# One visit a pair, on 64x64 quarters, for pairs 13 to 24 too

## The chip, the cores and the metric

The kernel runs on one core of a Trainium2 chip. The metric is the device time of the core in microseconds (us), a median over runs. The core's engines have a queue each and run it in order: TensorE (PE, matmuls), VectorE (DVE), ScalarE (ACT), GpSimd (POOL), and SyncE (SP), which issues DMAs.

## The reference

Attention with RMS-normalized queries and keys, followed by a feed-forward network with squared ReLU, in float32 (the weights arrive as float64):

```python
def _attn_ref(q, k, v, g_q, g_k):          # (8, 12, 448, 64) each
    rmsnorm = lambda x, g: x / np.sqrt(np.mean(x * x, axis=-1, keepdims=True) + 1e-06) * g
    q_n, k_n = (rmsnorm(q, g_q), rmsnorm(k, g_k))
    scores = 1.0 / np.sqrt(q.shape[-1]) * np.matmul(q_n, k_n.transpose(0, 1, 3, 2))
    attn = np.exp(scores - np.max(scores, axis=-1, keepdims=True))
    attn = attn / (np.sum(attn, axis=-1, keepdims=True) + 1e-09)
    return np.matmul(attn, v)
def _moe_ref(x, w_in, w_out):              # (3584, 768), (768, 2048), (2048, 768)
    h = np.maximum(x @ w_in, 0.0)
    return (h * h @ w_out)
# between them: x = attn_out.transpose(0, 2, 1, 3).reshape(3584, 768)
```

## The kernel before

**Work.** The 8 x 12 heads are 48 pairs of heads of one batch, 6 pairs a batch. The keys of a head are 448 = 3 x 128 + 64: three full slots and a half one, and the half slots of an even pair and of the odd pair behind it share one tile, scored with the even pair. Scores are made with keys on partitions. ACT turns them into weights with an exponential that applies the scale (`weigh`, L466), POOL adds a pair's weight tiles into one sum a head (`add_up`, L485), PE sums these over partitions by a matmul with ones (`denominators`, L620), DVE transposes the result (`take_sums`, L662) and inverts it (L679, L680). The values product (`attend`, L550, for the full slots; L586 for the half ones) is multiplied by that inverse in `finish`.

**Units.** The feed-forward network works on two batches at a time, a unit of four blocks. A block has first products (L1021 in the first unit, L1077 in later ones), whose results DVE combines (L1163) and ACT squares (L1169, L1170), sums of hidden parts on POOL (L1186), and second products (L1200 for the rest of the rows, L1286 for the others), whose results DVE adds up (L1383). The first unit uses seven products in place of eight; the later units go one level deeper. During the first unit the weights are converted as well: ACT (L1443 to L1446, "words") and DVE (L1457, L1476) make float32 of the words that DMAs bring, and DVE and POOL make their sums, the forms (L1552). DVE also makes sums of the input weights for the later units (L1512, "more").

**Visits.** Work on attention is done in visits between product passes. Pairs 0 to 12 are done alone, ahead of the first unit. The visit of pair i holds the scores of pair i and the values product of pair i - 1. For pairs 13 to 24, in the first unit, there are two visits a pair (`visit_among`), at every 24th of the unit's cost: in the first, slots 0 and 1 are attended (L550) and scored (L458), in the second the rest; the separate `denominators(i - 1)` stand half a step ahead of the second one, or in it where it is the unit's second step. From pair 25 on there is one visit (`visit_whole`), in which attending (L565) and scoring (L447) alternate slot by slot, each matmul cut into 64 by 64 quarters: the values product goes to two banks, one for the upper and one for the lower halves of the keys, which `join_halves` adds afterwards (L576 to L578). Denominators are made there for two pairs at once at the head of an even visit (`both_denominators`, L629).

**Banks.** The eight PSUM banks appear in the lists below as bank_172 to bank_179 (0 to 7). Products take turns on 5, 6 and 7 (`roles`). `visit_among` scores into banks 0 to 3, has the denominators in bank 3 and the values in bank 4. A whole visit has the values in 4 and 3, the denominators in 2, and scores into these pairs of banks:

```python
        if whole(i) and not shift:
            return [banks[n][:, 0:S] for n in ((0, 1), (2, 0), (1, 2), (0, 4))[m]]
```

**Order.** The Python code writes every engine's instructions in the order in which they run. Beside the visits, small work waits in `tasks` and `pool_tasks` and is written out piece by piece between product passes: normalization of a later pair (`prepare`: squares on ACT L181, means on DVE L194 and L197, the inverse root and the scaling on POOL L204 and L219), POOL's adds, inversion. Queries and keys of the next pair are turned by DVE (L370), the queries scaled by ACT (L380), then "qT" and "kT". `alone`, `shift` (a path for inputs whose scores need a maximum; it does not run here) and `whole` choose the form; `joint(i)` says that a pair's values product is made in quarters.

## Time and profile before

| | us |
|---|---|
| median of 3 runs | 1377.88 (1377.27 to 1378.17) |
| span of the profiled execution | 1376.2 |
| median less span | 1.7 |
| PE busy in the span | 1351.8 |
| DVE, ACT, POOL busy | 819.2, 614.6, 792.1 |
| PE busy in 110 to 290, 290 to 480 | 177.5 of 180, 187.5 of 190 |
| DVE, ACT, POOL busy in 290 to 480 | 140.5, 111.5, 120.9 of 190 |

The profiled execution has no time of its own beside its span; the times are those of three other runs. The span runs from its first to its last instruction. The first unit with pairs 13 to 24 lies at about 126 to 470 us of it. The granted clock of PE is 1.00 in both stretches. In the chain of waits a piece is a run of instructions that sets the end; in the timelines, brackets show how long the engine sat idle ahead of an instruction and whom it waited for.

### The profile page before, as it was taken

The numbers are of one execution on the slowest core, as the hardware profiler recorded it, in microseconds if no ns is written. First come the engines' busy times: TensorE is split into PE (matmuls) and PEld (weight loads), VectorE is DVE, ScalarE is ACT, GpSimd is POOL, SyncE is SP. The second block draws the span as 40 slices with busy tenths as digits, with TensorE's granted clock in tenths as the row PEclk, the third lists the DMA queues.
The fourth block names the chain that finished last, engine by engine and source line by source line (L and its number), as shares of the span: only waits on it lengthen the run. The fifth ranks groups of instructions, "written<-read, shape, count | busy, mean of one in ns | idle before, by whom it ended". The sixth has DMA issues, their size and how long they took to land.

```text
span 1376.2 us, 19610 instructions
## 1 busy us (share of the span) xinstructions
PE 1351.8 (98%) x6320; PEld 844.0 (61%) x6320; DVE 819.2 (60%) x1647; ACT 614.6 (45%) x1130; POOL 792.1 (58%) x792
## 2 busy tenths in 40 slices
PE   7999999999999999999999999999999999999998
PEld 3333444444444476677768586766767777868684
DVE  4897555877767765455547755455556642544454
ACT  6995476757757244442434244443524032203030
POOL 5668664755656878576767887565846630303030
PEclk9999999999999999999999999999999999999999
DMA  5665846977859866674748575665527441515133
GB/s 137 172 180 152 206 110 166 255 194 204 253 135 280 253 173 207 155 206 107 222 99 242 166 201 163 150 198 144 175 70 240 149 166 65 172 57 184 40 126 105
DMA packets 394372, 229.82 MB, mean 167 GB/s; under 512 B 271892, under 2 KB 355988, under 8 KB 393236
## 3 DMA queue, kind: packets, MB, share of 16 engines
q1 hardware_dynamic: 393968, 228.41, 58.8%
q8 instruction: 52, 0.85, 0.3%
q14 instruction: 60, 0.49, 0.1%
q10 hardware_dynamic: 292, 0.07, 0.0%
HBM read 171.05 MB, written 57.34 MB: 166 GB/s over the span
## 4 chain that ended last, share of the span: by engine, by line
PE 86%; DVE 3%; POOL 3%; issue 2%; ACT 2%; DMA 2%; SPq 1%; POOLq 0%; ACTq 0%; DVEq 0%
PE bank L1286 31%; PE bank L1077 25%; PE bank L1021 8%; PE bank L565 4%; PE bank L447 4%; PE bank L458 4%; PE bank L550 3%; PE bank L1200 2%; PE bank L586 1%; DMA in_sb<-in_deep 1%; PE bank L629 1%; PE bank L602 1%; PE bank L620 1%; DVE acc L1383 1%; SPq L159 1%
## 5 line engine op out<-in xcount | busy, mean ns | idle before, releaser
L1077 PE MATMUL bank<-xT,in_sb 128*128 128x224 f32 x1344 | 288.0, 353 | 0.0
L1286 PE MATMUL bank<-out_sb,hid 128*128 128x384 f32 x768 | 273.0, 488 | 2.0 <-POOL out_sb L1552 1.4
L1383 DVE TENSOR_TENSOR acc<-acc,bank 128x384 f32<-128x384 f32 x312 | 166.3, 548 | 160.0 <-PE bank L1286 131.4
L1077 PEld LDWEIGHTS bank<-xT,in_sb 128*128 128x128 f32 x1344 | 252.9, 190 | 10.4 <-ACT wT L466 5.6
L466 ACT ACTIVATE wT<-bank,rr 128x448 f32<-128x448 f32 x288 | 164.0, 632 | 157.9 <-PE bank L447 97.9
L1286 PEld LDWEIGHTS bank<-out_sb,hid 128*128 128x128 f32 x768 | 144.6, 190 | 104.4 <-issue 6.3
L1286 PE MATMUL bank<-out_sb,sums 128*128 128x384 f32 x576 | 207.0, 490 | 1.1 <-DVE acc L1383 0.7
L204 POOL TENSOR_TENSOR rr<-ms,minus_half 128x8 f32<-128x8 f32 (+1 forms) x96 | 145.3, 1514 | 69.1 <-DVE ms L197 65.8
L1062 DVE TENSOR_TENSOR hid<-hid,bank 128x224 f32<-128x224 f32 x312 | 111.3, 384 | 83.0 <-PE bank L1077 77.9
L1286 PEld LDWEIGHTS bank<-out_sb,sums 128*128 128x128 f32 x576 | 107.7, 190 | 86.0 <-DVE acc L1383 4.1
L1021 PE MATMUL bank<-xT,in_sb 128*128 128x448 f32 x336 | 131.7, 545 | 0.0
L485 POOL TENSOR_TENSOR sum<-sum,wT 128x448 f32<-128x448 f32 (+1 forms) x96 | 112.5, 1194 | 7.6 <-ACT wT L466 6.1
L458 PE MATMUL bank<-qT,kT 64*128 64x448 f32 (+1 forms) x492 | 102.4, 571 | 3.5 <-ACT qT L380 2.4
L1021 PEld LDWEIGHTS bank<-xT,in_sb 128*128 128x128 f32 x336 | 62.1, 190 | 68.8 <-issue 60.9
L1130 POOL TENSOR_TENSOR hid<-hid 128x448 f32<-128x448 f32 x24 | 27.3, 1144 | 123.1 <-DVE hid L1062 118.7
L485 POOL TENSOR_TENSOR sum<-wT 128x448 f32<-128x448 f32 x48 | 55.9, 1185 | 68.6 <-ACT wT L466 68.6
L1134 ACT ACTIVATE hid<-hid 128x448 f32<-128x448 f32 x96 | 55.0, 573 | 72.3 <-DVE hid L1062 48.4
L447 PE MATMUL bank<-qT,kT 64*64 64x448 f32 x552 | 75.1, 540 | 0.0
L1077 PE MATMUL bank<-more,in_sb 128*128 128x224 f32 x288 | 74.3, 353 | 0.0
L458 PEld LDWEIGHTS bank<-qT,kT 64*128 64x128 f32 (+1 forms) x492 | 35.3, 166 | 63.4 <-issue 37.1
L1074 ACT COPY hid<-bank 128x448 f32<-128x448 f32 x24 | 12.8, 533 | 136.9 <-PE bank L1077 136.1
L565 PE MATMUL bank<-wT,vt 64*64 64x448 f32 x576 | 73.3, 544 | 0.0
(142 smaller groups left out, 2063.1 us busy)
## 6 DMA issues: line engine op xcount, KB each, us to landing
out_sb<-out_forms SPq DMA_DIRECT2D x80, 384.0 KB, 5.2
in_sb<-in_deep SPq DMA_DIRECT2D x64, 384.0 KB, 4.1
in_sb<-in_deep SPq DMA_DIRECT2D x80, 256.0 KB, 4.2
words<-in_moe_w_in_dram SPq DMA_DIRECT2D x32, 384.0 KB, 3.9
words<-in_moe_w_out_dram SPq DMA_DIRECT2D x32, 384.0 KB, 3.6
out_forms<-out_sb SPq DMA_DIRECT2D x8, 1536.0 KB, 6.6
qk<-in_q_dram SPq DMA_DIRECT2D x96, 96.0 KB, 2.8
qk<-in_k_dram SPq DMA_DIRECT2D x96, 96.0 KB, 2.8
```

Source lines behind the costliest of these rows:

```text
L204: self.nc.gpsimd.tensor_tensor(out=self.rr[i][:, x, 0 : self.count(i)], in0=ms, in1=self.minus_half.to_broadcast(list(ms.shape)), op=ALU.pow,)
L447: nc.tensor.matmul(sc[ds(half * D, D)], lhsT=turned[i, 1][ds(e * D, D), ds(m * P + half * D, D)], rhs=turned[i, 0][ds(e * D, D), :], start ...
L458: nc.tensor.matmul(sc[some], lhsT=turned[p, 1][r, keys], rhs=turned[p, 0][r, :], start=True, stop=True,)
L466: nc.scalar.activation(new_weights((i, m), e), sc, AF.Exp, scale=rows.rr[i][:, 1, 2 * m + e : 2 * m + e + 1],)
L485: nc.gpsimd.tensor_tensor(out=sums[i, e][some], in0=left[some], in1=weights[key_of(i, m), e][some], op=ALU.add)
L565: nc.tensor.matmul(bank[ds(e * D, D), :], lhsT=values[i][keys, n, e, :], rhs=weights[(i, n), e][keys], start=n == 0, stop=n == NJ - 1 and ...
L1021: nc.tensor.matmul(ps, lhsT=w_sb[:, IN.index(left), c, :], rhs=forms[u, c][right], start=first and c == 0, stop=c == NK - 1, skip_group_ch ...
L1062: nc.vector.tensor_tensor(out=quarter(name, n), in0=quarter(base, n), in1=ps, op=ALU.add)
L1077: nc.tensor.matmul(ps, lhsT=left, rhs=right, start=start, stop=stop, skip_group_check=True)
L1134: nc.scalar.activation(dst, dst, AF.Relu)
L1286: nc.tensor.matmul(ps, lhsT=extra[left][:, t] if tt == NT else lefts[left][:, t, ts(tt, P)], rhs=w_sb[t][:, OUT.index(right), :], start=fi ...
L1383: nc.vector.tensor_tensor(out=acc, in0=acc, in1=ps, op=ALU.add)
```

## The change

`whole` becomes true from pair 13 on, so that pairs 13 to 24 get one visit each, where the first of their two visits stood. For them (`by_two` is false up to pair 23) the denominators of pair i - 1 stand at the head of visit i, with inversion and `finish` after it; from pair 24 on they go by two as before. `prepare` of pair i + 3 is written after a whole visit, where that of i + 2 followed a first visit; pair 15's is added to the alone visit of pair 12. `finish` of a joint pair multiplies on POOL (L708 before, L712 after) in place of DVE. No product pass, no weight conversion and no load is added or left out.

```diff
     def whole(i):
-        return i > 2 * 2 * NPAIR
+        return i > 2 * NPAIR
+
+    def by_two(i):
+
+        return i >= 2 * 2 * NPAIR
...
     def new_sum(i):
 
-        if i % 2 and whole(i):
+        if i % 2 and by_two(i):
             return new_part()
...
             if not alone(i) and not shift:
                 additions(i)
+            if whole(i + 1):
+                prepare(i + 3)
         begin(step + 1)
...
         else:
-            if i % 2 == 0:
+            if not by_two(i - 1):
+                denominators(i - 1)
+            elif i % 2 == 0:
                 both_denominators(i - 2)
...
             join_halves(i - 1)
+            if not by_two(i - 1):
+                tasks.append(lambda: invert(i - 1))
+                tasks.append(lambda: finish(i - 1))
+            elif i % 2 == 0:
+                tasks.append(lambda: invert_both(i - 2))
             if i % 2 == 0:
-                tasks.append(lambda: invert_both(i - 2))
                 if i <= last:
                     score(i, NJ)
                     weigh(i, NJ)
```

Lines of the changed kernel have numbers that are higher by 4 up to L1755 (L620 becomes L624, L662 L666, L1552 L1556).

On PE at the visit of pair 13, before (L1021 are product passes, L620 pair 12's denominators, bank_176 the values):

```order
L1021 MATMUL bank_178<-xT,in_sb 128x448 x3
L550 MATMUL bank_176<-wT,vt 64x448 x4
L458 MATMUL bank_172<-qT,kT 128x448
L458 MATMUL bank_173<-qT,kT 128x448
L458 MATMUL bank_174<-qT,kT 128x448
L458 MATMUL bank_175<-qT,kT 128x448
L1021 MATMUL bank_177<-xT,in_sb 128x448 x3
L1021 MATMUL bank_179<-xT,in_sb 128x448 x3
L1021 MATMUL bank_178<-xT,in_sb 128x448 x3
L620 MATMUL bank_175<-sum,ones 64x448 x2
L550 MATMUL bank_176<-wT,vt 64x448 x2
L586 MATMUL bank_176<-wT,lasts_156 64x448 x2
```

and after:

```order
L1025 MATMUL bank_178<-xT,in_sb 128x448 x3
L624 MATMUL bank_174<-sum,ones 64x448 x2
L569 MATMUL bank_176<-wT,vt 64x448 x2
L569 MATMUL bank_175<-wT,vt 64x448 x2
L451 MATMUL bank_172<-qT,kT 64x448 x2
L451 MATMUL bank_173<-qT,kT 64x448 x2
L569 MATMUL bank_176<-wT,vt 64x448 x2
L569 MATMUL bank_175<-wT,vt 64x448 x2
L451 MATMUL bank_174<-qT,kT 64x448 x2
L451 MATMUL bank_172<-qT,kT 64x448 x2
```

The denominators stand ahead of the whole visit, where a first visit and three rows of product passes stood ahead of them, and the scores of slot 1 go to their bank.

On DVE around the visit of pair 17, before (L1512, L1476, L1552 and L1457 are work on weights, L1163 the hidden parts, L662 pair 16's denominators):

```order
L1163 TENSOR_TENSOR hid<-bank_178,part 128x448
L1512 TENSOR_TENSOR more<-in_sb 128x512
L1552 TENSOR_TENSOR out_sb<-out_sb 128x384
L1476 ISA out_sb<-words,out_sb 128x768
L1512 TENSOR_TENSOR more<-in_sb 128x384
L1457 TENSOR_SCALAR out_sb<-words 128x384
L194 TENSOR_REDUCE ms<-squares 128x6
L197 TENSOR_SCALAR ms<-ms 128x6
L1163 TENSOR_TENSOR hid<-bank_177,part 128x448
```

and after, where bank_174 is pair 16's denominators:

```order
L374 STREAM_TRANSPOSE kT<-qk_65 128x448
L374 STREAM_TRANSPOSE qT<-qk_65 128x448
...
L1167 TENSOR_TENSOR hid<-bank_178,part 128x448
L1516 TENSOR_TENSOR more<-in_sb 128x512
L1556 TENSOR_TENSOR out_sb<-out_sb 128x384
L1480 ISA out_sb<-words,out_sb 128x768
L666 STREAM_TRANSPOSE inverse<-bank_174 128x448
L582 TENSOR_TENSOR xT<-xT,bank_175 128x448
L1516 TENSOR_TENSOR more<-in_sb 128x384
```

The same work on weights runs up to the same L1476 (L1480), and the transpose of the denominators, with the join of the quarters behind it, now stands directly behind it; before, nine rows stood between it and L662.

On POOL at the turn from first to second products ahead of the visit of pair 18, before (L1186 are the sums of hidden parts, L485 pair 17's adds, L1552 the forms of the output weights, L204 and L219 pair 20's normalization):

```order
L1186 TENSOR_TENSOR sums<-hid,sums 128x384
L1186 TENSOR_TENSOR hid<-hid 128x384
L485 TENSOR_TENSOR sum<-wT 128x448 x2
L1552 TENSOR_TENSOR out_sb<-out_sb 128x384
L485 TENSOR_TENSOR sum<-sum,wT 64x448 x2
L1552 TENSOR_TENSOR out_sb<-out_sb 128x384
L485 TENSOR_TENSOR sum<-sum,wT 128x448 x2
L1552 TENSOR_TENSOR in_sb<-in_sb 128x384
L204 TENSOR_TENSOR rr<-ms,minus_half 128x8
```

and after:

```order
L489 TENSOR_TENSOR sum<-sum,wT 128x448 x2
L1190 TENSOR_TENSOR sums<-hid 128x384
L1190 TENSOR_TENSOR sums<-sums,hid 128x384
L1190 TENSOR_TENSOR sums<-hid,sums 128x384
L1190 TENSOR_TENSOR hid<-hid 128x384
L204 TENSOR_TENSOR rr<-ms,minus_half 128x8
L219 TENSOR_TENSOR qk_64<-qk_64,rr 128x512
L204 TENSOR_TENSOR rr<-ms,minus_half 128x8
L1556 TENSOR_TENSOR out_sb<-out_sb 128x384 x2
```

Pair 17's adds move ahead of the hidden sums, and pair 20's normalization ahead of the two forms.

## The prediction

> **What bounds the kernel now.** I read the page first (busy shares, the chain that ended last), then the chain of waits through the first unit (110 to 480 us) and the start of the second, where visits already have the new form, and then the engines' timelines at the places where the chain leaves PE.

> ```profile
> span 1376.2 us, 19610 instructions
> PE 1351.8 (98%) x6320; PEld 844.0 (61%) x6320; DVE 819.2 (60%) x1647; ACT 614.6 (45%) x1130; POOL 792.1 (58%) x792
> PE 86%; DVE 3%; POOL 3%; issue 2%; ACT 2%; DMA 2%; SPq 1%; POOLq 0%; ACTq 0%; DVEq 0%
> ```

> PE is busy for 98% of the span, so only two things count: how long PE's own work lasts, and any wait put in front of it. The median of the runs, 1377.88 us, is 1.7 above this span; I add that at the end.

> In the chain of waits one pair (15) of the first unit looks like this, with columns start, length, piece:

> ```profile
> 187.66 1.65 PE bank L550 x8
> ...
> 191.02 5.36 PE bank L1286 x16
> 196.38 0.90 PE bank L620 x4
> 197.28 5.36 PE bank L1286 x16
> 202.64 0.90 PE bank L550 x4
> ...
> 205.41 10.52 PE bank L1286 x32
> ```

> A first visit of 3.36 us (187.66 to 191.02), denominators of 0.90, a second visit of 2.77 (202.64 to 205.41): 7.03 in three interruptions of the product stream. The stream also pays for each. 16 passes take 5.36 and 32 take 10.52, so a pass costs 0.3225, and 5.36 less 16 of these leaves 0.20 per restart.

> In the second unit a visit is whole; an odd and an even one:

> ```profile
> 483.36 0.91 PE bank L565 x8
> ...
> 485.78 1.02 PE bank L447 x8
> ...
> 489.06 2.09 PE bank L1077 x10
> ...
> 502.53 0.89 PE bank L629 x8
> ...
> 509.09 10.98 PE bank L1077 x57
> ```

> The odd one lasts 5.70 and holds no denominators; with the 0.90 that the first unit's form has, 6.60. The even one, denominators included, lasts 6.56.

> **What the change removes.** (1) Interruptions. Pairs 13 to 24 have 12 first visits, 12 second ones and 11 separate denominators, 35 in all; 12 remain. 23 x 0.20 = **4.6 us**. (2) Shorter visits: 7.03 against 6.6, 12 times: **5.1**. (3) The first unit's even pairs score the keys left over of both pairs in their second visit, and PE waits there for the next pair's queries:

> ```profile
> 172.08 1.92 PE L458 MATMUL bank<-qT,kT 64*128 64x448 f32 x8
> 174.89 0.97 PE L458 MATMUL bank<-qT,kT 64*64 64x448 f32 x4 [0.89 <-ACT qT L380]
> 175.79 0.59 PE L1200 MATMUL bank<-out_sb,hid 128*128 128x384 f32 x1
> 353.13 0.97 PE L458 MATMUL bank<-qT,kT 64*64 64x448 f32 x4 [1.49 <-ACT qT L380]
> ```
> ```profile
> 232.76 2.58 PE bank L458 x12
> 292.50 1.86 PE bank L458 x12
> 411.00 2.58 PE bank L458 x12
> ```

> Undisturbed this takes 1.86 (292.50). Pair 14 takes 3.71, 1.85 too long; pair 20, whose wait is 0.60 longer, 2.45; pairs 16 and 22 0.72 each: **5.7** in all. In the changed order both turned blocks of the next pair are made ahead of the visit's exponentials on DVE and ACT, half a visit's distance earlier, so I let all of it go (bounds 2.9 and 5.7). Together 15.4.

> **What it adds: three waits.** First, **visit 13**. Its denominators, those of pair 12, stood 10 us behind the visit's head and now open it. What they need is made by POOL:

> ```profile
> 131.74 2.66 POOL L742 TENSOR_TENSOR xT<-xT 128x448 f32<-128x448 f32 x2 [1.44 <-DVE xT L715]
> 134.37 2.21 POOL L485 TENSOR_TENSOR sum<-wT 128x448 f32<-128x448 f32 x2
> 136.54 5.84 POOL L485 TENSOR_TENSOR sum<-sum,wT 128x448 f32<-128x448 f32 x4
> ```
> ```profile
> 131.61 1.66 PE bank L550 x8
> ...
> 141.93 1.08 PE bank L620 x3
> ```

> The change does not move these adds: on POOL they stay behind the L742 pair, which waits for DVE. The head stands at 131.61, and even before PE took L620 only at 141.93, as the adds were ending (142.38). Everything that covered this, the first visit and 18 passes, is now queued behind the denominators on PE. The wait is 141.93 - 131.61 = 10.3; with PE idle DVE has less to do beside POOL, and the four adds at the 1.11 of the two before them instead of 1.46 would end 1.4 sooner: 8.9. I take **9.7**.

> Second, **visits 17, 20 and 23**, the second of a block whose weights are being converted meanwhile. Bank 2 now holds the denominators, and the scores of slot 1 need it: from the rows above 0.90 + (485.78 - 483.36) = 3.3 us behind the head. It comes free when DVE transposes it (L666 of the changed kernel), which in DVE's order stands behind all that ran up to here, and behind one more transpose of queries:

> ```profile
> 241.22 0.68 DVE L1512 TENSOR_TENSOR more<-more,in_sb 128x512 f32<-128x512 f32 x1
> ...
> 245.01 2.15 DVE L1512 TENSOR_TENSOR more<-in_sb 128x512 f32<-128x512 f32 x1
> ...
> 252.59 1.35 DVE L1512 TENSOR_TENSOR more<-in_sb 128x384 f32<-128x384 f32 x1
> ...
> 430.85 1.35 DVE L1512 TENSOR_TENSOR more<-in_sb 128x384 f32<-128x384 f32 x1
> ```
> ```profile
> 246.81 1.65 PE bank L550 x8
> ...
> 425.05 1.65 PE bank L550 x8
> ```

> Head 246.81, the work ahead done at 252.59, two transposes of about 0.63: 253.9, or 7.1 behind the head. 7.1 - 3.3 = 3.8. Visit 23 (425.05, 430.85) gives the same, and visit 20 has the same instructions ahead. One of them will be faster: the L1512 of 2.15 ran while POOL made an add, where its like took 0.68.

> ```profile
> 244.27 2.33 POOL L485 TENSOR_TENSOR sum<-sum,wT 64x448 f32<-64x448 f32 x2
> ```

> A visit's adds now come in one run soon after it, so this one is gone by then: 3.8 - 1.5 = 2.3. If the three other operations slowed in that stretch became fast too (two of 1.35 where 0.55 is usual, one of 0.96 for 0.68), 0.4 would be left. I take 2.7 each, **8.1** in all (bounds 1.2 and 11.4). [...]

> Third, **the turn from first to second products** ahead of visits 18, 21 and 24. There a second visit of 2.77 stands on PE, which the change takes away, and POOL's last two forms of the output weights must come:

> ```profile
> 274.09 0.91 PE L1286 MATMUL bank<-out_sb,hid 128*128 128x384 f32 x2 [0.33 <-DVE acc L1383]
> 275.71 0.91 PE L1286 MATMUL bank<-out_sb,hid 128*128 128x384 f32 x2 [0.71 <-POOL out_sb L1552]
> ```
> ```profile
> 267.14 1.01 POOL L1186 TENSOR_TENSOR hid<-hid 128x384 f32<-128x384 f32 x1
> ...
> 274.65 1.01 POOL L1552 TENSOR_TENSOR out_sb<-out_sb 128x384 f32<-128x384 f32 x1
> ...
> 287.05 1.77 POOL L204 TENSOR_TENSOR rr<-ms,minus_half 128x8 f32<-128x8 f32 x1
> ...
> 291.82 1.07 POOL L1552 TENSOR_TENSOR in_sb<-in_sb 128x384 f32<-128x384 f32 x1
> ```

> Before, PE would get to these passes at 273.8 without the wait, now 2.8 earlier, at 271.0. POOL is free of the hidden sums at 268.1 in both. What then came first was adds and forms by turns; now it is the normalization of pair 20 (L204, L219, L204: 287.05 to 291.82, 4.8), and the two forms of 1.0 end at 273.9 and 274.9. The second pair of passes would begin at 271.7 and begins at 274.9: 3.2. Visit 24 has this order too; ahead of 21 one form stands in front of the normalization and only the other behind it, 2.3 by the same sum. 8.7 in all, less the waits that were there, 0.33 + 0.71 twice: **6.6** (bounds 0, if POOL gets to the normalization earlier, and 10).

> Nothing else reaches PE by my reading. The other heads find their denominators ready: a visit's adds and POOL's new product (L712) are some 9 to 11 us of POOL, and 18 or more us of product passes lie between visits. The moved normalizations and loads come earlier than before, behind the products.

> **The sum.** 15.4 gained, 9.7 + 8.1 + 6.6 = 24.4 lost: span 1376.2 + 9.0 = 1385.2, time **1386.9**. This case's own range: 1381 to 1393.

> **Rivals.** *DVE and POOL keep up; only visit 13 waits.* Since adds are gone from the stretch where DVE ran slowly, and POOL's normalizations may run ahead of the hidden sums, the second and third waits go to their lower bounds, 1.2 and 0: 9.7 + 1.2 - 15.4 = -4.5, time **1373.4**, faster. For it speaks that DVE's slow operations stand beside POOL's; against it the in-order queues, in which the awaited instruction comes last. It decides if L666 ends within 3.3 us of the heads of 17, 20 and 23.

> *One of the two goes.* Without the second wait +0.9, without the third +2.4: **1378.8 or 1380.3**, hardly to be told from no change. For it speaks that the second hangs on about 4 us of DVE, the third on 3 of POOL, independently.

> *Reading the banks becomes the bound.* ACT must take six exponentials in a visit of 6.6 us where it had four and two, and DVE's join of the quarters waits for the visit's end with weight conversions queued behind it. If each of the nine other visits costs 1 us by this, +18: **1396**. In the second unit such a visit shows the L447 at 485.78 stretched from 0.75 to 1.02, no more, but ACT converts no weights there. [...]

> *The tiles give nothing in this unit*, if the quarters' 6.6 is reached only beside deep products: 5.1 less, about 1392, inside the first case's range.

> **Chances and range.** The forecast (the last rival in it) 0.52, all slower. Only visit 13 waits 0.18: faster 0.14, the same 0.04. One of the two goes 0.19: the same 0.15, slower 0.04. The banks 0.11, slower. A measurement here tells 0.2%, some 2.8 us, from no change; so faster 0.14, the same 0.19, slower 0.67. The range leaves out most of the fast case and of the slowest: 1375 to 1395.

> **What will show it.** On PE: L624 at about 131.6 with a wait of 9 to 10 us on POOL's sum; L451 at 17, 20 and 23 waiting 2 to 4 us on DVE's L666; L1290 ahead of 18, 21 and 24 waiting 2 to 3 us on POOL's L1556; no wait on ACT's qT; visits of 6.6 us, product chunks with one restart between them. I am wrong if the adds of pair 12 come early enough, if DVE reaches L666 soon after the head, or if a head other than 13's waits for POOL.

## The result, and the profile after

The changed kernel takes 1410.17 us (median of four runs, 1408.77 to 1411.93) where the kernel before took 1378.03 beside it (1377.27 to 1378.28): a ratio of 1.0234, 95% interval 1.0220 to 1.0249. It is 32 us slower. The forecast was 1386.9, range 1375 to 1395: the sign was right and the size was not. One run of a version below took 1992.84 us at a granted clock of 0.66 and is left out of its median.

The profiled execution took 1409.54 us. Three lines of its page:

```profile
span 1407.4 us, 20180 instructions
PE 1352.2 (96%) x6608; PEld 855.0 (61%) x6608; DVE 823.2 (58%) x1647; ACT 619.2 (44%) x1136; POOL 807.1 (57%) x804
PE 78%; DVE 8%; issue 4%; DMA 3%; POOL 3%; SPq 2%; ACT 1%; POOLq 0%; DVEq 0%; ACTq 0%
```

PE's share of the chain fell from 86% to 78% and DVE's rose from 3% to 8%. The span is 31.2 longer, and all of it arises in the stretch from the head of visit 13 (131.6 before, 131.8 after) to the end of visit 25 (489.06 before, 520.30 after); behind it both run alike. That stretch in the view by windows, first of the kernel before, then of the changed one (from:to and length; busy time and count of PE, PE's weight loads, DVE, ACT and POOL; granted clock; DMA share; GB/s):

```profile
131.60:489.06 357.46, 353.05 (x1214) 162.84 (x1213) 246.06 (x434) 220.28 (x384) 226.32 (x191) 1.00 0.74 202
```
```profile
131.60:520.30 388.70, 353.98 (x1502) 174.13 (x1501) 252.74 (x436) 226.22 (x392) 246.27 (x209) 0.97 0.69 187
```

PE's idle time, length less busy time, is 4.4 before and 34.7 after: +30.3. Its busy time hardly moved, though the change was to save some of it. The reason is in the clock: 0.97. Taken in windows of 1 us, busy time times (1 - clock) sums to 9.7 us. So the work by itself shrank by 353.05 - (353.98 - 9.7) = 8.8, and running at half clock ate it up. That is this execution; the mean granted clock of all four runs was 0.988 to 0.991.

What PE waited for between 126 and 521, by line and releaser (total us, times, longest), before and after:

```profile
PE bank L458 <- ACT qT L380: 2.4, 2, 1.5
PE bank L1286 <- POOL out_sb L1552: 1.4, 2, 0.7
PE bank L1286 <- DVE acc L1383: 0.6, 2, 0.3
```
```profile
PE bank L1290 <- DVE acc L1387: 11.2, 10, 2.6
PE bank L624 <- POOL sum L489: 8.7, 1, 8.7
PE bank L451 <- DVE inverse L666: 8.6, 3, 3.1
PE bank L1290 <- POOL out_sb L1556: 2.2, 2, 1.5
PE bank L1204 <- ACT hid L1174: 2.1, 2, 1.4
PE bank L451 <- ACT wT L470: 1.4, 1, 1.4
PE bank L1290 <- DVE acc L1311: 0.4, 1, 0.4
```

The second and third rows are the two first waits of the prediction, in the place and nearly the size given. The largest row was not in it: PE waits ten times for DVE to add a bank of second products to `acc`. On PE's timeline of the changed kernel (start, length, engine, line, operation, tiles, shapes, count; in brackets the idle time ahead and its releaser) the predicted waits are:

```profile
140.49 2.84 PE L624 MATMUL bank<-sum,ones 128*64 128x448 f32 x4 [8.72 <-POOL sum L489]
...
258.29 1.06 PE L451 MATMUL bank<-qT,kT 64*64 64x448 f32 x6 [3.13 <-DVE inverse L666]
...
353.68 0.97 PE L451 MATMUL bank<-qT,kT 64*64 64x448 f32 x4 [2.47 <-DVE inverse L666]
...
451.95 0.98 PE L451 MATMUL bank<-qT,kT 64*64 64x448 f32 x8 [3.02 <-DVE inverse L666]
```

and two of those at the turns from first to second products ahead of visits 18 and 24:

```profile
282.94 2.24 PE L1290 MATMUL bank<-out_sb,hid 128*128 128x384 f32 x4 [2.61 <-DVE acc L1387]
...
481.64 1.65 PE L1290 MATMUL bank<-out_sb,hid 128*128 128x384 f32 x2 [1.46 <-POOL out_sb L1556]
```

A visit itself became what was forecast. Two pieces of the chain of waits, the head of an odd visit and the first products behind it, are 6.67 apart:

```profile
195.01 0.90 PE bank L624 x4
...
201.68 20.84 PE bank L1290 x64
```

The lag behind the kernel before, taken at the heads of the visits, is 9.9 us at 14, shrinks to 6.6 at 16, and jumps at 18 (13.5), 21 (20.5) and 24 (28.5): once per block, at each turn, beside the waits at 17, 20 and 23.

Why DVE is late, on its timeline ahead of L666 at visit 17 and then at the wait of 2.61:

```profile
252.98 0.73 DVE L1461 TENSOR_SCALAR out_sb<-words 128x384 uint32<-128x384 uint32 x1 [2.12 <-ACT words L1447]
...
255.05 1.34 DVE L1556 TENSOR_TENSOR out_sb<-out_sb 128x384 f32<-128x384 f32 x1
256.32 1.36 DVE L1480 CUSTOM_DVE_ANT_0 out_sb<-words,out_sb 128x768 uint16<-128x768 uint16 x1
257.60 0.64 DVE L666 STREAM_TRANSPOSE inverse<-bank 128x448 f32<-128x448 f32 x1
...
277.98 0.69 DVE L194 TENSOR_REDUCE ms<-squares 128x8 f32<-128x512 f32 x1 [1.38 <-ACT squares L181]
278.70 0.92 DVE L197 TENSOR_SCALAR ms<-ms 128x8 f32<-128x8 f32 x1
279.54 0.54 DVE L1516 TENSOR_TENSOR more<-in_sb 128x384 f32<-128x384 f32 x1
280.01 1.34 DVE L1556 TENSOR_TENSOR out_sb<-out_sb 128x384 f32<-128x384 f32 x1
281.28 1.14 DVE L1461 TENSOR_SCALAR in_sb<-words 128x384 uint32<-128x384 uint32 x1
282.34 1.01 DVE L1387 TENSOR_TENSOR acc<-acc,bank 128x384 f32<-128x384 f32 x2
```

L666 stands behind two operations on the coming block's weights (L1556, L1480), and a little ahead of them DVE had stood idle for 2.12 us until a conversion on ACT was done; the add that PE awaits (L1387) stands behind a normalization (L194, L197) and three more on weights (L1516, L1556, L1461). This small work is given out by product passes: the program counts `spent`, the cost of the passes issued, and writes a piece when its due number is reached. Before, a pair's passes were cut into three stretches by the interruptions on PE, in which nothing new was given out. Now they stand in one. On ACT, between 181 and 378 us, the conversions (L1443) started 2.4 to 8.4 us apart before, with one gap of 13.0. Now (L1447) a gap of 10 to 14 us lies at each of the visits 16 to 20 (220.4 to 232.0, 256.3 to 266.6, 287.9 to 297.9, 313.8 to 328.1, 353.1 to 365.2), and the pieces come between them.

DVE did not become slower in all: over the whole stretch its operations on weights (L1476, L1457, L1512, L1552) last 119.2 us before and 118.9 after. What changed is when they come.

### The profile page after: what moved, and what is told of

Its sections match the earlier page's. It is cut to its first block, busy times and chain, and to the rows that moved or that the text cites. A ratio compares the mean times of both kernels' runs of the same rounds, so it can differ in the third digit from the quotient of the medians.

```text
span 1407.4 us, 20180 instructions
## 1 busy us (share of the span) xinstructions
PE 1352.2 (96%) x6608; PEld 855.0 (61%) x6608; DVE 823.2 (58%) x1647; ACT 619.2 (44%) x1136; POOL 807.1 (57%) x804
## 4 chain that ended last, share of the span: by engine, by line
PE 78%; DVE 8%; issue 4%; DMA 3%; POOL 3%; SPq 2%; ACT 1%; POOLq 0%; DVEq 0%; ACTq 0%
PE bank L1290 29%; PE bank L1081 25%; PE bank L451 6%; PE bank L569 6%; PE bank L1025 4%; PE bank L462 2%; PE bank L1204 2%; DVE acc L1387 1%; PE bank L590 1%; PE bank L554 1%; PE bank L624 1%; PE bank L633 1%; POOL rr L204 1%; DVE more L1516 1%; DVE out_sb L1480 1%
## 5 line engine op out<-in xcount | busy, mean ns | idle before, releaser
L1081 PE MATMUL bank<-xT,in_sb 128*128 128x224 f32 x1344 | 287.9, 353 | 0.1
L1290 PE MATMUL bank<-out_sb,hid 128*128 128x384 f32 x768 | 275.3, 490 | 12.4 <-DVE acc L1387 9.8
L1081 PEld LDWEIGHTS bank<-xT,in_sb 128*128 128x128 f32 x1344 | 252.9, 190 | 10.5 <-ACT wT L470 5.8
L1387 DVE TENSOR_TENSOR acc<-acc,bank 128x384 f32<-128x384 f32 x312 | 165.7, 547 | 129.6 <-PE bank L1290 118.7
L1290 PEld LDWEIGHTS bank<-out_sb,hid 128*128 128x128 f32 x768 | 144.6, 190 | 115.8 <-DVE acc L1387 15.1
L1290 PE MATMUL bank<-out_sb,sums 128*128 128x384 f32 x576 | 207.9, 492 | 2.5 <-DVE acc L1387 2.0
L204 POOL TENSOR_TENSOR rr<-ms,minus_half 128x8 f32<-128x8 f32 (+1 forms) x96 | 146.3, 1524 | 64.7 <-DVE ms L197 62.1
L1290 PEld LDWEIGHTS bank<-out_sb,sums 128*128 128x128 f32 x576 | 108.4, 191 | 87.4 <-issue 5.5
L451 PE MATMUL bank<-qT,kT 64*64 64x448 f32 x840 | 119.6, 551 | 10.1 <-DVE inverse L666 8.6
L1025 PE MATMUL bank<-xT,in_sb 128*128 128x448 f32 x336 | 128.7, 542 | 0.0
L569 PE MATMUL bank<-wT,vt 64*64 64x448 f32 x864 | 113.4, 551 | 0.0
L582 DVE TENSOR_TENSOR xT<-xT,bank 128x448 f32<-128x448 f32 x36 | 22.4, 621 | 102.1 <-ACT xT L581 99.5
L451 PEld LDWEIGHTS bank<-qT,kT 64*64 64x64 f32 x840 | 45.8, 134 | 55.8 <-issue 38.2
L384 ACT ACTIVATE qT<-qT,g 128x448 f32<-128x448 f32 x34 | 22.6, 665 | 121.3 <-DVE qT L374 121.3
```

Source lines behind the costliest of these rows:

```text
L204: self.nc.gpsimd.tensor_tensor(out=self.rr[i][:, x, 0 : self.count(i)], in0=ms, in1=self.minus_half.to_broadcast(list(ms.shape)), op=ALU.pow,)
L451: nc.tensor.matmul(sc[ds(half * D, D)], lhsT=turned[i, 1][ds(e * D, D), ds(m * P + half * D, D)], rhs=turned[i, 0][ds(e * D, D), :], start ...
L569: nc.tensor.matmul(bank[ds(e * D, D), :], lhsT=values[i][keys, n, e, :], rhs=weights[(i, n), e][keys], start=n == 0, stop=n == NJ - 1 and ...
L1025: nc.tensor.matmul(ps, lhsT=w_sb[:, IN.index(left), c, :], rhs=forms[u, c][right], start=first and c == 0, stop=c == NK - 1, skip_group_ch ...
L1081: nc.tensor.matmul(ps, lhsT=left, rhs=right, start=start, stop=stop, skip_group_check=True)
L1290: nc.tensor.matmul(ps, lhsT=extra[left][:, t] if tt == NT else lefts[left][:, t, ts(tt, P)], rhs=w_sb[t][:, OUT.index(right), :], start=fi ...
```

## The experiments

Times are medians, ratios are to the kernel before on the same chip, with 95% intervals. The diffs are against the changed kernel except where the kernel before is named.

**One wait taken away.** Only the denominators of pair 12 are moved three steps behind visit 13.

```diff
             if not by_two(i - 1):
-                denominators(i - 1)
+                if not (i - 1 == 2 * NPAIR):
+                    denominators(i - 1)
...
+        if not shift and not by_two(i - 1) and (i - 1 == 2 * NPAIR):
+            tasks.extend([gap] * 3)
+            tasks.append(lambda: denominators(i - 1))
+            tasks.append(lambda: invert(i - 1))
+            tasks.append(lambda: finish(i - 1))
```

> The changed kernel with one edit: pair 12's denominators (with inversion and finish) come three product steps behind pair 13's visit instead of at its head; pairs 13 to 23 as in the change. Theory W (the head's wait is the cost, and PE runs at half clock for some 3 us behind a long wait): the 8.7 us wait goes, with the 1.6 us that the half clock cost there (140.5 to 143.4), and one restart of 0.2 comes: about 10 us less than the change, 1400 us. Rival L (the other engines are what is late; PE's wait here only lets them catch up): the next waits grow, and less than 5 us are won, 1405 to 1410 us.

Measured: 1407.67, ratio 1.0226 (1.0202 to 1.0249): 2.5 less than the change, which the intervals hardly tell from nothing, and not 10. The wait of 8.7 is gone, and others have come. Three of this kernel's waits in the same stretch:

```profile
PE bank L451 <- ACT wT L470: 4.0, 4, 1.5
PE bank L1025 <- DVE hid L1167: 3.1, 1, 3.1
...
PE bank L569 <- DMA vt<-in_v_dram: 1.5, 1, 1.5
```

The head of visit 13 stands 9.2 us earlier than in the change, that of 14 3.8, that of 16 0.8, and that of 18 at 290.2 in both. Something other than PE sets the pace there. My theory that each wait costs its own length fell with this run.

**All denominators behind the visit.** The same edit with `True` for the condition on the pair.

> All first-unit denominators (pairs 12 to 23) three product steps behind the visit instead of at the next visit's head. Theory W: besides the 10 us of pair 12, the three waits for DVE's L666 (8.6 us) and the 1.4 us for ACT at pair 20's visit go, with the half clock behind the first two (1.7 and 3.0 us), and twelve restarts (2.4) come: about 22.5 us less than the change, 1388 us. Rival D (DVE is late by itself, because it stands idle for the join of the quarters, 55 us in the twelve visits): the lateness moves to DVE's accumulations (11.2 us of PE's waits, which then grow), about 12 us less than the change, 1398 us.

Measured: 1429.79, 1.0371 (1.0354 to 1.0389), 20 us more than the change; neither theory had it. The waits for L624 and L666 are gone, those for `acc` grew to 20.2, those for `hid` to 4.1, for weights on ACT to 7.4, for a load of V to 7.5, and half clock costs 15.8. The edit also puts three gaps ahead of other small work, so it doesn't say which order did it; I leave its cause open.

**One visit without quarters and join.** The banks of the scores and of the half slots are changed to suit; these lines are left out here.

```diff
-        return whole(i - i % 2 + 1) and not shift
+        return i - i % 2 + 1 > 2 * 2 * NPAIR and whole(i - i % 2 + 1) and not shift
...
-        if whole(i) and m < NJ:
+        if whole(i) and by_two(i - 1) and m < NJ:
...
-            join_halves(i - 1)
+            if joint(i - 1):
+                join_halves(i - 1)
```

> One visit a pair with the denominators at its head as in the change, but on the tiles of before (values with all 128 keys into one bank, scores 128 keys at a time), so that there is no join: the values are read by DVE later, in finish. Theory D (the join holds DVE): DVE's 55 us of waiting in the visits go, the PE waits for DVE's accumulations (11.2) and for L666 (8.6) fall to a third, 13 us less, against 12 visits longer by 0.2 to 0.4 us (4): about 1401 us. Theory W: waits stay, the visits are longer, 1412 to 1415 us.

Measured: 1417.1, 1.0289 (1.0272 to 1.0306). The waits are for the most part those of the change (`acc` 10.5, POOL's sum 8.7, L666 6.6; 29.4 in all, where the change has 34.6). So the loss is there without the quarters and the join; merging the visits brings most of it, and what of the other 5.2 belongs to the join this run doesn't tell. The quarters give back 7 us. In the trace PE's work at full clock is 8.1 longer without them, and half clock costs 14.1 in place of 9.7.

**PE kept busy through the wait at visit 13.** First 18 matmuls of no use ahead of the denominators, then 11, since 18 ran 4 us past the wait.

```diff
+            if i == 2 * NPAIR + 1:
+                for _ in range(11):
+                    nc.tensor.matmul(
+                        banks[1][ds(0, D), 0:S], lhsT=ones, rhs=turned[i, 1], start=True, stop=True,
+                    )
             if not by_two(i - 1):
```

> The change with 18 matmuls of no use (ones by pair 13's keys, into bank 1, which is overwritten) ahead of pair 12's denominators, some 8 us of PE work in the 8.7 us in which PE waited there. If the half clock behind the wait (0.50 from 137 to 143 us) comes from PE's idleness, it is 1.00 there and the four L624 passes take 0.90 instead of 2.84: 1.6 to 2 us less, 1408 us. If it comes from something else, nothing changes, 1410 us.

> The filling of x4 with 11 matmuls instead of 18, since each of its passes took 0.375 us and not 0.225: 22 passes, 8.3 us, in the 8.7 us wait. If idleness sets the half clock: 1.00 from 132 to 150 us, pair 13's visit ends 1.6 us sooner than in the change (147.6 against 149.2); the time hardly moves by theory C. If not: 149.2 again.

Measured: with 18, 1414.33, 1.0248 (1.0224 to 1.0272), of no use for the time; with 11, 1408.76, 1.0227 (1.0206 to 1.0247). By windows, the change and then the kernel with 11 (the number ahead of the DMA share is the clock):

```profile
136.00:138.00 2.00, 0.00 (x0) 0.00 (x0) 1.24 (x3) 0.00 (x0) 2.00 (x3) 0.72 0.59 126
138.00:140.00 2.00, 0.00 (x0) 0.00 (x0) 1.45 (x1) 0.00 (x0) 2.00 (x2) 0.50 0.50 114
140.00:142.00 2.00, 1.51 (x3) 0.57 (x4) 0.00 (x0) 0.00 (x0) 2.00 (x3) 0.50 0.40 111
142.00:144.00 2.00, 2.00 (x11) 0.41 (x12) 0.64 (x1) 0.00 (x0) 1.92 (x3) 0.57 0.93 277
144.00:146.00 2.00, 2.00 (x26) 0.74 (x20) 0.01 (x1) 0.68 (x2) 1.00 (x1) 1.00 0.97 291
```
```profile
138.00:140.00 2.00, 1.92 (x6) 0.43 (x4) 1.21 (x1) 0.00 (x0) 2.00 (x2) 1.00 0.50 114
140.00:142.00 2.00, 1.64 (x4) 0.38 (x4) 0.00 (x0) 0.00 (x0) 2.00 (x3) 1.00 0.53 145
```

The busy PE kept its clock at 1.00 through the same stretch; the idle one lost half of it from about 137 and had it back shortly before 144. The products behind visit 13 begin 1.2 us sooner (147.92 for 149.16). The time is 1.4 less, which the intervals don't tell from nothing.

**The conversions spread over the visits too.** A visit counts for the due numbers like product passes (52 units of cost), due pieces may be written between a visit's slots, and all are due 20 units earlier.

```diff
-        block + 2 + every * (n - 2 * tile_pieces) for n in range(len(all_pieces) - ahead)
+        (block + 2 + every * (n - 2 * tile_pieces)) * (1 if shift else 1 + 12 * 52 / COST) - (0 if shift else 20)
+        for n in range(len(all_pieces) - ahead)
...
+    def tick():
+        if first and not shift:
+            visited[0] += 52 / 3
+            follow_loads()
+            end_join()
+            while pieces_due and pieces_due[0] <= spent + visited[0]:
+                pieces_due.popleft()
+                convert()
...
-            while first and late and late[0] <= spent:
+            while first and late and late[0] <= spent + visited[0]:
...
                     weigh(i, n)
+                tick()
```

> The change with the conversion of the weights paced by the visits too: of the four pieces a pair (each a DMA, three ACT operations, two DVE operations) about one is now written inside the visit, between its slots, and the stretch of product passes behind it has fewer. Theory C (the conversions are what is late: they stood in three gaps of the first unit's pairs and now must all be made in one stretch of 18 us, while DVE and ACT stand idle for the visit): PE's waits for DVE (acc 11.2, L666 8.6) fall by half or more, about 15 us less than the change, 1395 us. Rival B (DVE and ACT are held by the visit's own join and exponentials, whatever the conversions do): pieces inside the visit delay the exponentials as well, no gain, 1408 to 1415 us.

Measured: 1391.54, 1.0100 (1.0083 to 1.0117): 18.6 of the 32 us gone by the order of the same instructions. PE's waits:

```profile
PE bank L1290 <- DVE acc L1387: 10.7, 9, 2.2
PE bank L624 <- POOL sum L489: 8.7, 1, 8.7
PE bank L451 <- ACT wT L470: 2.2, 2, 1.1
PE bank L1204 <- ACT hid L1174: 1.5, 1, 1.5
PE bank L1290 <- ACT acc L1383: 0.5, 1, 0.5
```

The waits for L666 and POOL's forms are gone, and half clock, 9.7 before, costs 2.5, all of it at visit 13. 8.6 + 2.2 + 7.2 = 18.0, nearly the whole gain. By the heads of visits 15 to 22 one piece more has been started than in the change (two at 20), so the run doesn't tell the spreading from the earlier start; both are the pace. The waits for `acc` stayed, which I had expected halved. On DVE, ahead of the add for the turn at 18, stands

```profile
279.67 0.69 DVE L194 TENSOR_REDUCE ms<-squares 128x8 f32<-128x512 f32 x1 [3.48 <-ACT squares L181]
```

DVE is idle there for 3.48 us: its queue is held by a normalization that waits for ACT.

**Less work per conversion.** First the addition on DVE that completes each converted piece is left out, then one of ACT's three steps too, and the first of these in the kernel before as a control.

```diff
-            nc.vector.tensor_tensor(out=bits, in0=bits, in1=both[:, :, 0], op=ALU.add)
```
```diff
-        nc.scalar.activation(low.bitcast(F32), low, AF.Copy, scale=2.0**-29, bias=2.0**23)
```

> The change without the second DVE operation of each conversion (L1480, 0.55 to 1.5 us each, 64 times): the low bits of the weights are left out, so the output is a little off. Theory C with DVE as the late member: DVE gets some 45 us of work less in the unit, its waits on PE's path (acc, L666) fall to a few us and the half clock behind them goes: 20 us less than the change, 1390 us. Rival M (DMAs of the words through three buffers, and SP's queue, are the late member): the pieces arrive as before, less than 6 us won, 1404 to 1410 us.

> As the run before, and without one of the three ACT operations of each conversion too (L1448, the low word, 0.46 to 0.57 us each): ACT gets 22 us of work less in the unit. If ACT is late as well, 5 us or more less than the run without L1480; if DVE alone, the same within 2 us.

> The kernel before without the second DVE operation of each conversion (L1476), as a control: PE waited for DVE 1.2 us there, so by every theory that holds DVE's lateness for a thing of the change nothing happens, 1376 to 1379 us. If it becomes faster by 5 us or more, DVE's conversions cost time before the change as well.

Measured: without the addition 1388.51, 1.0081 (1.0065 to 1.0098), 21.7 less than the change; without ACT's step as well 1390.78 (median of three), 1.0082 (1.0062 to 1.0102), nothing more; the control 1374.31, 0.9976 (0.9966 to 0.9987), 3.4 less than the kernel before, where I had expected none. One operation of DVE per piece is worth 21.7 us in the changed kernel and 3.4 in the other. So the conversions were late in the changed order and had room in the old one. Two things stay open. In the profiled executions half clock costs 9.0 us without ACT's step and 1.7 with it (mean clocks 0.990 and 0.997); with that taken off, the spans are 1380.7 and 1383.9, so some 3 us by ACT may be hidden. And the addition left out also frees the buffer of the words sooner: ACT's waits for their loads are 21.9 us before, 24.7 after the change, 13.6 here and 1.7 with the conversions spread. No run tells DVE's own time from these loads.

**The sums of pair 12 on PE.** Visit 13 adds them up by matmuls and needs nothing of POOL; first in the changed kernel, then with the conversions spread.

```diff
-            if not alone(i) and not shift:
-                additions(i)
...
-            if not by_two(i - 1):
+            if i == 2 * NPAIR + 1:
+                add_weights(i - 1, range(NJ + 1))
+                take_sums(i - 1)
+            elif not by_two(i - 1):
                 denominators(i - 1)
```

> The change, with pair 12's sums made by PE from the weights themselves (16 passes with ones, as for the pairs before it; 1.64 us instead of 0.90) in place of POOL's adds and L624, so that nothing at pair 13's head waits for POOL. Theory W: the wait of 8.7 us and its half clock of 1.6 go, 0.7 comes: 9.6 us less than the change, 1400.5 us. Theory C (the conversions of the weights, on DVE above all, are late; PE's wait at the head only lets them catch up): the heads of pairs 14 and 15 come up to 9 us sooner, that of pair 18 within 1 us of where it was; less than 4 us won, 1406 to 1410 us.

> The edit of the run before together with the paced conversions of x5 (1391.5). With DVE no longer late by the conversions, the time won at pair 13's head stays won: by both theories 8 to 10 us less than x5, 1382 to 1384 us. If DVE is late still (its acc waits were 10.7 us in x5), 3 to 5 us, 1387 us.

Measured: alone 1403.7, 1.0194 (1.0172 to 1.0217), 6.5 less than the change, between the two theories; the head of visit 18 stands 6.2 sooner, where the second theory had at most 1. Its two largest waits:

```profile
PE bank L451 <- DVE inverse L666: 12.1, 4, 3.3
PE bank L1290 <- DVE acc L1387: 11.2, 10, 2.6
```

Of the 8.7 taken away, 3.5 came back at once as a fourth wait for L666. With the conversions spread: 1385.91, 1.0066 (1.0049 to 1.0083), 5.6 less than spread alone, and no half clock in the profiled execution (mean clocks of the four runs 0.996 to 0.999). What PE then still waits for:

```profile
PE bank L1290 <- DVE acc L1387: 10.7, 9, 2.2
PE bank L451 <- DVE inverse L666: 3.3, 1, 3.3
PE bank L451 <- ACT wT L470: 2.1, 2, 1.1
PE bank L1204 <- ACT hid L1174: 1.5, 1, 1.5
PE bank L1290 <- ACT acc L1383: 0.5, 1, 0.5
```

18.1 of waits where the kernel before has 4.4, less 8.8 of saved work: 4.9 more, and the span is 5.5 longer (1381.7).

**What is left: the join, the normalization, the pace.** Three edits on top of that kernel: the join of an odd visit's quarters a step later; the normalizations at pairs 17, 20 and 23 eight steps later; and visits counted double (104 for 52).

```diff
-            join_halves(i - 1)
+            if i % 2 and not by_two(i - 1):
+                tasks.append(gap)
+                tasks.append(lambda: join_halves(i - 1))
+            else:
+                join_halves(i - 1)
```
```diff
+        behind = 8 if first and not shift and i in (17, 20, 23) else 0
         if shift or i % 2:
-            prepare(i + 3)
+            prepare(i + 3, behind)
         else:
-            tasks.append(lambda: tasks.append(lambda: prepare(i + 3, 0)))
+            tasks.append(lambda: tasks.append(lambda: prepare(i + 3, behind)))
```
```diff
-            visited[0] += 52 / 3
+            visited[0] += 104 / 3
```

> As the run before, and in the visits of odd pairs the join of the quarters (two ACT copies, L582 on DVE) is written one product step later, behind work on weights. Theory J (DVE's standing idle for the join, 37 us in x5's odd visits, is a cost of its own): DVE waits some 15 us less there, PE's acc waits fall from 10.7 by half, 5 us less than the run before. If only the amount of work between visits counts: the same within 1.5 us.

> x10 (paced conversions, pair 12's sums by PE; 1385.9), and in the second visit of blocks 2 to 4 (pairs 17, 20, 23) the normalization of the pair three further on is written eight steps later, behind the turn to the second products. Theory N (its means, which wait for ACT's squares, hold DVE and POOL ahead of the accumulations and forms): the acc waits at the turns (2.2 and 2.1 us) and ACT's hid (1.5) go, some 5 us less, 1380 to 1381 us. If the accumulations are late by the amount of DVE's work alone, the waits stay, 1385 to 1387 us.

> x10 with the visits counted double in the pacing (104 units of cost instead of 52), so that about two of the four pieces a pair fall into the visit. If the conversions between the visits are what is left of DVE's lateness: acc waits fall below 6 us, 1381 us. If the visit becomes the bound (exponentials behind the words on ACT): waits for ACT in the visits, 1388 to 1395 us.

Measured: join 1385.18, 1.0057 (1.0040 to 1.0074), the same as without it, so DVE's hold at the join (its waits at L582 fell from 38.6 to 9.8) costs nothing of its own in this kernel. Normalization 1384.39, 1.0047 (1.0032 to 1.0061): the waits for `acc` fell from 10.7 to 5.1 as the theory said, but 5.3 for L666 and 1.7 for queries stand in their place, and 1.5 us are gained where 5 were expected. Pace 1382.2, 1.0033 (1.0022 to 1.0044), the best of all versions, with

```profile
PE bank L1290 <- DVE acc L1387: 5.8, 7, 1.5
PE bank L451 <- DVE inverse L666: 4.0, 2, 3.6
PE bank L451 <- ACT wT L470: 3.2, 5, 0.7
...
```

A repeat of the normalization kernel, and the edits together:

> The same kernel once more on this chip, as a measure of how far two builds of the same kernel lie apart: within 1.5 us of x13.

> x15 (conversions paced with the visits counted double, pair 12's sums by PE; 1382.2) with the late normalization of x13. If DVE's and ACT's lateness is one sum of work ahead of PE's need, the two add up: PE's waits fall to 8 us, 3 to 5 us less, 1377 to 1379 us, level with the kernel before. If waits only change place: 1381 to 1384 us.

> x16 with the late join of x11 as well (which changed nothing there, 1385.2 against 1385.9): the same as x16 within 1.5 us, unless the join is what holds DVE once the rest is gone, then 2 to 4 us less.

Measured: 1385.04, 1.0051 (1.0032 to 1.0070), within 0.7 of the first time; pace and normalization together 1384.17, 1.0044 (1.0030 to 1.0057), no better than either; with the late join as well 1389.18, 1.0081 (1.0068 to 1.0095), 5 us worse, which I had not expected. Near the optimum the edits don't add up. No version beats the kernel before, and what the last 4.5 us hang on stays open: each edit made one wait smaller and another larger.

## Why the prediction was right or wrong

**The gains, 15.4.** Fewer interruptions and shorter visits were put at 4.6 + 5.1 = 9.7 of PE's work; 8.8 was measured at full clock. The third gain, the waits for the next pair's queries, was put at 5.7 from lengths of chain pieces, and of these 2.4 were recorded waits. Those are gone; the other 3.3 are not to be found in the rows. So 11.2 was gained, 4.2 short, and 3.3 of that by this step, where I had a lower bound of 2.9 and passed it over.

**First, visit 13: 9.7.** Measured 8.7, by the mechanism named. Its price was mistaken in another way: taking it off brought 2.5, 6.5 and 5.6 us in three runs. A PE that comes sooner meets the next late engine sooner: in the second and third run, 3.5 and 3.3 us came back as a further wait for L666.

**Second, visits 17, 20, 23: 8.1.** Measured 8.6 (3.13, 2.47, 3.02), as named. The slow operations did not go with POOL's adds, as the lower figure there (2.3 each) had it, and it came out further off. The two ahead of L666 in the rows above still take 1.34 and 1.36, where the first one's size takes 0.54 in the row at 279.54. POOL was making sums of hidden parts beside them (L1190, 254.54 to 255.98 and 255.94 to 257.26), and each ends 0.4 us behind one of these. Which of POOL's work would stand beside them was misread.

**Third, the turn: 8.7 gross.** Measured 11.4 (3.3 ahead of 18, 2.7 ahead of 21, 5.3 ahead of 24), at the place named but by other hands: POOL's forms hold PE for 2.2 in all, the rest is DVE's `acc` and ACT's `hid`.

**"Nothing else reaches PE by my reading" is the step that failed, and with it the price of a wait.** Another 6.0 us of waits, for `acc` elsewhere and for ACT's weights, had no term, nor had DVE and ACT at the turns. I had counted POOL's work per visit against the 18 us between visits, and DVE only up to L666. DVE's and ACT's small work per run of passes was not counted, though the change takes away two of the three interruptions in which it was caught up with. That its pace sets most of the loss is shown from two sides: written at another pace, 18.6 us go; with one operation fewer, 21.7 go, of which the old order gives only 3.4. The first of these took away the waits for L666 and for POOL's forms, which had terms, and most of the half clock. The waits for `acc`, which had none, stayed at 10.7 there and fell only with the later normalization (5.1) or the wider pace (5.8).

**The clock had no term.** A wait was priced at its own length. Half clock behind the waits cost 9.7 more, the largest single miss.

The sum by these steps: 8.7 + 8.6 + (11.4 - 2.0 that were there before) + 6.0 + 9.7 - 11.2 = 31.2, the 31.2 of span. The forecast's sum was 9.0. Of the 22.2 between them 9.7 are the clock, 6.0 the other waits, 2.8 the turns and 4.2 the missing gains; the first two waits take 0.5 off.

**The rivals.** That only visit 13 waits, or one of two goes, fell with the rows for L666 and the turns. Of "Reading the banks becomes the bound" one clause was right, that weight conversions queue up on DVE; what it blamed was not: without quarters and join the loss is larger, the join a step later changes nothing in the spread kernel, and one step fewer on ACT brings no time. The exponentials did not hold PE for long either: its waits for them (L451 for `wT`) are 1.4 us. That the tiles give nothing fell with the 7 us for the quarters.

## What to carry to other kernels

Where small work is paced by another engine's stream, a change of that stream's cuts is a change of the small work's schedule: count it anew, for every engine, per stretch between the places where it can catch up. A cover that is taken away does not leave one wait but brings the next late queue to the front, so removing one wait on trial undervalues it while another engine is late, and several small fixes don't add up. Here a wait on TensorE had to be priced with the clock behind it: half clock cost 9.7 of the 31.2 us, and runs of one kernel differed in it (mean clocks of 0.991 to 0.997 with 18 matmuls of no use).

## What the runs showed of the hardware

The granted clock fell to 0.50 some 5 us into the wait of 8.72 and stayed there for about 3 us after PE began again. It also fell behind waits of 3.13 (260 to 263), 2.61 (284 to 287), 2.47 with 1.44 behind it (355 to 362) and 0.93 with 1.46 behind it (482 to 485), but not behind that of 3.02 at 451.95, where the windows show 1.00 throughout. In the changed kernel half clock never stood without a wait ahead of it, and the PE kept busy with 11 matmuls of no use did not lose its clock in the same place (1.00 from 130 to 150).
